# Loads of three value units issued later, four output products moved ahead of a score block, and two x copies put on one engine

## The chip, the cores and the metric

The kernel runs on one core of a Trainium2 chip. The metric is the device time of one launch in microseconds. The engines are TensorE (PE in the profile, with its weight loads as PEld), VectorE (DVE), ScalarE (ACT), GpSimd (POOL) and SyncE (SP), which here only starts DMA transfers. Each engine takes its instructions in the order in which they stand in its own queue, and waits on semaphores for the others.

## The reference

Sliding-window attention is followed by a feed-forward block. q, k and v have 8 batches, 8 heads, 576 positions and 64 elements. Masks keep the scores within 32 positions.

```
scores = scale * (q @ k^T);  scores = -1e9 where |i - j| > 32
attn   = softmax(scores)
x      = (attn @ v), heads side by side         # 4608 tokens x 512
h      = x @ w_in                               # 512 -> 2048
g      = h * sigmoid(1.702 * h)
out    = g @ w_out                              # 2048 -> 512, float32
```

## The kernel before

The 4608 tokens are cut into 36 units of 128 queries and 9 tiles of four units (512 tokens). A unit's queries start 32 positions after its keys, so each unit of queries meets the keys of its own unit and the first half of the next.

**Attention of a unit `u`.** `scores(u, tag)` (or `scores_two` for a pair) multiplies keys and queries into PSUM banks, and ScalarE takes the exponential into `p`. `band` multiplies `p` by the window's mask on VectorE (`band_two` for a pair). `values(u, tag)` multiplies `p` by the values; a ones column gives the softmax sum. `norm` divides on VectorE and leaves the unit in `xn`. `values_four` and `norm_four` do the same for four units. Then x is transposed into `xT`, which is the moving operand of layer one: `x_T2(u, tag, eng)` transposes two units on TensorE into one bank, and the engine `eng` copies them out; `x_T` without a bank asks SP for a DMA transpose. The first three tiles use TensorE, the later ones SP.

**Values.** `load_v(u)` is a DMA issued by GpSimd into one of nine buffers `ve`. The values' second block of 128 keys starts 64 positions later, so `odd_v(u, eng)` makes a copy `vo` shifted by half a unit: its first instruction copies the upper half of `ve[u]`, its second the lower half of `ve[u + 1]`, and so it waits for the load of `u + 1`. Queries and keys of later units come by `load_kq`, also issued by GpSimd (`ahead("kq", u)` loads q of `u` and k of `u + 1`), and `turn` asks SP for their DMA transposes. SP's queue holds, in order, these transposes, the output stores, and the transposes of x.

**Layers one and two.** Both are multiplied by a scheme of seven block products in place of eight (numbers 1 to 7 in the code), with sums of blocks made on VectorE: `x_sums` makes `xs` from `xT`, `g_sums` makes `gs` from `g`. A group of layer one (`l1_group`) takes the banks A, C, B and E; VectorE adds in PSUM (L592, L598), ScalarE copies (L68) and takes the activation (L579). The products of layer two are a list of closures, here called `more` and `l2`, of which `do(more, n)` issues the next `n`. They fill TensorE between dependent steps.

**Order.** The order is written out by hand in `run`, `first_layer1`, `front` and `back`. The change lies between layer one of the second tile (`first_layer1`, units 4 to 7) and that of the third (`back(2)`, units 8 to 11, beside which units 12 to 15 get their values). The PSUM banks are named "A", "B", "C", "E", the double bank "t", and "LA", "LB" for layer two. The probabilities `p` of a pair of units take one of two buffers, so that units 12 and 13 use the one of units 8 and 9 again.

In later stages GpSimd is paced by a copy of one element into the tile `seen`, which makes it wait until that element's tile is written:

```
self.nc.gpsimd.tensor_copy(self.seen, self.gs[t - (n == 0)][0:1, 2, c, 255:256])
```

Of the kernel before, what the change touches and what calls it, by code (L numbers as in the profile page):

```python
# [26 lines left out]
class _Kernel:  # L27
# [844 lines left out]
    @staticmethod  # L872
    def do(fs, n=99):
        for _ in range(min(n, len(fs))):
            fs.pop(0)()
# [76 lines left out]
    def run(self):  # L952
        pool, act = self.nc.gpsimd, self.nc.scalar
        self.l2eng, self.seed2 = self.nc.vector, act
        more = self.l2 = self.layer2_plain(0, 0) + self.layer2([(i, j) for i in range(self.NT) for j in range(2)][1:-1],
                                                               (self.NT - 1, 1))
        self.opening()
        self.do(self.x_sums(1))
        late = self.first_layer1()
        do = self.do  # L960
        dve = self.nc.vector
        do(more, 8)
        self.scores_two(8, ("t", "AC"))
        exps = self.scores(10, "BE", True)
        self.turn(14)
        self.turn(15)
        do(late)
        do(more, 4)
        self.band_two(8)
        self.l2eng = act  # L970
        do(more, 16)
        do(exps)
        do(more, 8)
        self.values(8, "t")
        self.values(9, "AC")
        self.odd_v(12, pool)
        self.odd_v(13, pool)
        self.ahead("kq", 16)
        self.scores(11, "BE")
        self.norm(8)  # L980
        self.band(10)
        self.norm(9)
        do(more, 12)
        self.scores_two(12, ("t", "BE"))
        self.values(10, "AC")
        self.band(11)
        self.norm(10)
        do(more, 6)
        self.values(11, "t")
        self.norm(11)  # L990
        self.scores(14, "BE")
        self.x_T2(8, "A", act)
        do(more, 4)
        self.x_T2(10, "C", dve)
        self.scores(15, "t")
        do(more, 6)
        do(self.x_sums(2))
        self.seed2 = self.l2eng = dve
        self.odd_v(14, pool)
        self.odd_v(15, pool)  # L1000
        late = self.back(2)
        for t in range(3, self.NT):
            self.front(t, late)
            late = self.back(t)
        self.l2eng = act
        self.do(late, 2)
        self.do(self.l2, 16)
        self.do(late)
        self.do(self.l2, 999)

    def first_layer1(self):

        def b(*which):
            return [lambda i=i, j=j: self.w2_sums((i,), j) for i, j in which]

        dv = b((3, 0), (3, 1), (1, 0), (1, 1))
        extra = {0: [lambda: self.w1_sums((4,), 1), lambda: self.g0_sum(1)] + b((2, 0), (2, 1)), 1: b((4, 0), (4, 1)),
                 2: [lambda: self.g0_sum(2)], 3: []}
        for n in range(4):
            self.odd_v(8 + n, self.nc.gpsimd)  # L1020
            self.ahead("kq", 12 + n)
            for u in ((), (), (), (13, 14, 15, 16))[n]:
                self.load_v(u)

            chunks = ((1, 2, 3, 3), (1, 1, 3, 5), (2, 2, 8, 4), (2, 2, 6, 6))[n]
            sums = ((0, 0, 1, 1, 2), (3, 1, 0, 1, 3), (1, 0, 2, 1, 2), (2, 1, 1, 0, 1))[n]

            def fill(i):
                at = (1, 7, 2, 4).index(i)
                self.do(self.l2, chunks[at])  # L1030
                self.do(dv, {1: sums[0], 7: sums[1], 2: 0, 4: sums[4]}[i])
                if i == 7 and n:
                    self.T_pe([("k8", "q8", "k9"), ("q9", "k10", "q10"), ("k11", "q11", "k12")][n - 1], self.nc.scalar)
                    if n == 3:
                        self.turn(12)
                        self.turn(13)

            self.l1_group(1, n, fill, lambda i: self.do(dv, sums[2 + i]))
            dv += self.g_sums(1, 2 * n, 2) + extra[n]
        return dv  # L1040
# [46 lines left out]
```

## Time and profile before

| | us |
|---|---|
| median of 3 runs | 279.73 |
| lowest, highest run | 278.90, 280.01 |
| the profiled execution | 278.88 |
| its span | 277.1 |
| TensorE busy | 265.1 |
| VectorE busy | 213.7 |
| ScalarE busy | 196.1 |
| GpSimd busy | 140.2 |

The span runs from the first to the last record; the execution's own time has 1.78 us around it. In a row of a timeline stand the start, the length, the engine, the line of the kernel, the operation, what it writes and reads, and how many were merged. Idle time ahead of the row and what ended it stand in brackets. Most matmuls have line 71 and most copies line 68, which are helpers, so the tile names tell the steps apart: `sc` are scores, `pv` values, `tp` transposes, `h` layer one, `o` layer two. TensorE's matmuls are pipelined, so that a row's end lies beyond the start of the next. Times are counted from the span's start.

### The profile page before, as it was taken

Reading aid. Unit: us, or ns where it says so; the run is one execution under the profiler, and the core shown is the slowest. Engines: PE = TensorE matmul, PEld = TensorE weight load, DVE = VectorE, ACT = ScalarE, POOL = GpSimd, SP = SyncE. Lnnn points to the kernel's source line nnn. Section 1 sums busy time; section 2 is a strip of 40 time slices with the busy share of each in tenths; the row PEclk is TensorE's granted clock in tenths of the full one; section 3 lists DMA queues with packets and bytes.
Section 4 is the critical chain, followed back from the end, with each engine's and each line's share of the span. In section 5 each row is a group of like instructions: output and inputs, shape, how many; then the busy total and the mean of one; then the engine's idle time right before and its main releaser. Section 6 shows DMA issues by size and latency. Waiting matters only on the chain.

```text
span 277.1 us, 8812 instructions
## 1 busy us (share of the span) xinstructions
PE 265.1 (96%) x3604; PEld 222.4 (80%) x3604; DVE 213.7 (77%) x496; ACT 196.1 (71%) x346; POOL 140.2 (51%) x218
## 2 busy tenths in 40 slices
PE   1989999999999999999999999999999999999994
PEld 1568556888788888888888888888888888888883
DVE  4655998987888788888878887888788878856621
ACT  2586985999896689669956985698569766577320
POOL 8995597999693189729642974294430000000000
PEclk9999999999999999999999999999999999999999
DMA  8999999999999999999999999999992023202033
GB/s 86 165 199 199 180 207 166 164 150 149 188 133 212 163 122 165 173 198 120 171 171 172 151 167 181 134 141 125 153 120 80 0 89 65 78 0 78 0 117 116
DMA packets 151353, 37.74 MB, mean 136 GB/s; under 512 B 138640, under 2 KB 146960, under 8 KB 151312
## 3 DMA queue, kind: packets, MB, share of 16 engines
q0 software_dynamic: 107200, 18.42, 95.4%
q1 hardware_dynamic: 43664, 18.23, 34.3%
q8 instruction: 28, 0.46, 0.7%
q10 hardware_dynamic: 448, 0.52, 0.6%
q14 instruction: 13, 0.11, 0.1%
HBM read 36.83 MB, written 9.44 MB: 167 GB/s over the span
## 4 chain that ended last, share of the span: by engine, by line
PE 93%; ACT 2%; DMA 2%; DVE 1%; issue 1%; POOLq 0%
PE o L71 41%; PE h L71 40%; PE sc L71 5%; PE pv L71 4%; DMA kq<-in_k_dram 2%; PE tp L180 1%; PE tp L259 1%; ACT kq L68 1%; PE tp L463 1%; ACT p L340 1%; DVE xn L398 1%; ACT L803 0%; PE tp L204 0%; DVE kq L68 0%; PE tp L451 0%
## 5 line engine op out<-in xcount | busy, mean ns | idle before, releaser
L579 ACT ACTIVATE g<-h 128x512 f16<-128x512 f32 x128 | 72.1, 598 | 37.9 <-PE h L71 31.6
L71 PEld LDWEIGHTS <-g 128*128 128x128 f16 x568 | 54.6, 98 | 7.7
L71 PE MATMUL h<-xs,a 128*128 128x256 f16 x384 | 57.6, 272 | 0.0
L71 PEld LDWEIGHTS <-a 128*128 128x128 f16 x512 | 49.7, 98 | 8.4 <-DVE xs L495 0.3
L71 PE MATMUL h<-xT,w 128*128 128x256 f16 (+1 forms) x352 | 53.6, 283 | 0.0
L71 PEld LDWEIGHTS <-w 128*128 128x128 f16 x480 | 46.0, 98 | 8.6
L71 PE MATMUL o<-w,g 128*128 128x256 f16 (+1 forms) x304 | 49.9, 284 | 0.0
L233 POOL COPY vo<-ve 64x264 int32<-64x264 int32 x71 | 35.6, 502 | 18.0 <-DMA ve<-in_v_dram 14.5
L71 PEld LDWEIGHTS <-gs 128*128 128x128 f16 x416 | 39.9, 98 | 5.3
L71 PE MATMUL o<-b,gs 128*128 128x256 f16 x280 | 43.3, 273 | 0.0
L71 PE MATMUL o<-b,g 128*128 128x256 f16 x264 | 38.6, 273 | 0.0
L592 DVE TENSOR_TENSOR h<-h,s 128x512 f32<-128x512 f32 x32 | 22.4, 699 | 18.8 <-PE h L71 18.2
L214 POOL DMA_DIRECT2D ve<-in_v_dram x39 | 33.2, 864 | 2.5 <-issue 1.2
L144 POOL DMA_DIRECT2D qst<-in_q_dram x35 | 28.2, 808 | 1.3 <-issue 0.9
L598 DVE TENSOR_TENSOR h<-h,s 128x512 f32<-128x512 f32 x32 | 22.3, 698 | 7.3 <-PE h L71 7.1
L144 POOL DMA_DIRECT2D kst<-in_k_dram x31 | 26.6, 861 | 1.4 <-DMA w<-in_moe_w_out_dram 1.4
L68 ACT COPY h<-h 128x512 f32<-128x512 f32 x32 | 18.8, 587 | 10.4 <-PE h L71 9.6
L293 ACT ACTIVATE p<-sc 128x512 bf16<-128x512 f32 x48 | 24.7, 623 | 0.3 <-PE sc L71 0.2
L943 POOL COPY seen<-gs 1x1 f16<-1x1 f16 x17 | 3.3, 196 | 36.9 <-DVE gs L510 36.9
L68 ACT COPY o_sb<-o 128x256 f32<-128x256 f32 (+1 forms) x25 | 11.7, 467 | 12.6 <-PE o L71 12.6
L68 ACT COPY s<-h 128x512 f32<-128x512 f32 x32 | 19.1, 598 | 0.8
L71 PE MATMUL h<-xs,w 128*128 128x256 f16 x128 | 19.2, 273 | 0.0
(101 smaller groups left out, 389.0 us busy)
## 6 DMA issues: line engine op xcount, KB each, us to landing
out_dram<-o_sb SPq DMA_DIRECT2D x33, 256.0 KB, 4.1
ve<-in_v_dram POOLq DMA_DIRECT2D x31, 128.0 KB, 6.5
kst<-in_k_dram POOLq DMA_DIRECT2D x25, 128.0 KB, 5.7
qst<-in_q_dram POOLq DMA_DIRECT2D x21, 128.0 KB, 5.2
w<-in_moe_w_out_dram POOLq DMA_DIRECT2D x4, 512.0 KB, 10.6
w<-in_moe_w_in_dram POOLq DMA_DIRECT2D x4, 256.0 KB, 8.5
w<-in_moe_w_in_dram POOLq DMA_DIRECT2D x2, 512.0 KB, 10.6
qst<-in_q_dram POOLq DMA_DIRECT2D x7, 96.0 KB, 5.8
```

The source lines that it names most:

```text
L68: (eng.copy if eng is self.nc.scalar else eng.tensor_copy)(out, in_)
L71: self.nc.tensor.matmul(out, lhsT, rhs, start=start, stop=stop, skip_group_check=True)
L144: self.nc.gpsimd.dma_start(t[off:off + n], src[b, :, s:s + n, :].rearrange("h s d -> s h d"))
L180: self.nc.tensor.transpose(tp[64 * (h % 2):64 * (h % 2) + 64, h // 2, x, :], src[:, 4 * i + h, at + x, :], self.ident[r, r])
L214: self.nc.gpsimd.dma_start(t[off:off + n, :, :self.D], self.v[b, :, s:s + n, :].rearrange("h s d -> s h d"))
L233: eng.tensor_copy(*((words(vo[64:128]), words(self.ve[u % 9][64:128])), (words(vo[0:64]), words(nxt)))[i])
L259: self.nc.tensor.transpose(tp[:, i, hp, :], src[:, 128 * hp:128 * hp + 128], self.ident)
L293: exps = [lambda eo=eo: self.nc.scalar.activation(p[:, eo].rearrange("k h s -> k (h s)"), sc[eo], AF.Exp, scale=self.scale) for eo in rang ...
L579: act.activation(g[:, f, 256 * half:256 * half + 256], bank.rearrange("p (i n) -> p i n", i=2), AF.Gelu_apprx_sigmoid)
L592: dve.tensor_add(e, b, s7)
L598: dve.tensor_add(c, b, s7)
L943: self.nc.gpsimd.tensor_copy(self.seen, self.gs[t - (n == 0)][0:1, 2, c, 255:256])
```

## The change

The change has three parts.

The loads of values 14, 15 and 16 are issued later. They stood right behind that of 13 at the end of `first_layer1`. Now GpSimd first makes the odd copy of unit 12, copies one element of the masked probabilities of units 8 and 9 into `seen`, and then issues them, followed by q of 16 and k of 17. The odd copy of unit 13 moves behind those, to the odd copies of 14 and 15.

Four products of layer two, which stood between the two x copies of the third tile, are issued ahead of the scores of unit 14.

The copy of units 8 and 9 out of bank A goes to VectorE, where that of units 10 and 11 was already.

```
         self.values(9, "AC")
         self.odd_v(12, pool)
-        self.odd_v(13, pool)
-        self.ahead("kq", 16)
         self.scores(11, "BE")
         self.norm(8)
+        pool.tensor_copy(self.seen, self.pair[8][0:1, 0, 1, 0, 0:1])
+        for u in (14, 15, 16):
+            self.load_v(u)
+        self.ahead("kq", 16)
         self.band(10)
...
         self.norm(11)
+        do(more, 4)
         self.scores(14, "BE")
-        self.x_T2(8, "A", act)
-        do(more, 4)
+        self.x_T2(8, "A", dve)
         self.x_T2(10, "C", dve)
         self.scores(15, "t")
         do(more, 6)
         do(self.x_sums(2))
         self.seed2 = self.l2eng = dve
-        self.odd_v(14, pool)
-        self.odd_v(15, pool)
+        for u in (13, 14, 15):
+            self.odd_v(u, pool)
...
-            for u in ((), (), (), (13, 14, 15, 16))[n]:
+            for u in ((), (), (), (13,))[n]:
                 self.load_v(u)
```

GpSimd's queue around the end of `first_layer1`, with the difference marked. The tiles `ve_86` to `ve_89` hold the values of units 13 to 16, `ve_85` those of 12; `vo_93` is the odd copy of 12, and `vo_94` that of 13.

```order
-L214 DMA ve_87<-in_v_dram 128x8x64
-L214 DMA ve_88<-in_v_dram 128x8x64
-L214 DMA ve_89<-in_v_dram 128x8x64
 L233 COPY vo_93<-ve_85 64x264
 L233 COPY vo_93<-ve_86 64x264
+L979 CAST seen<-p 1x1
+L214 DMA ve_87<-in_v_dram 128x8x64
+L214 DMA ve_88<-in_v_dram 128x8x64
+L214 DMA ve_89<-in_v_dram 128x8x64
+L144 DMA qst<-in_q_dram 128x8x64
+L144 DMA kst<-in_k_dram 128x8x64
 L233 COPY vo_94<-ve_86 64x264
```

The three loads of values stand behind the odd copy of unit 12 and the new copy into `seen`, and the loads of q and k now stand ahead of the odd copy of unit 13.

TensorE's queue at the end of the values of unit 11 (`vo_92` is its odd copy) and the start of the scores of unit 14, with the difference marked:

```order
 L71 LDWEIGHTS p
 L71 MATMUL pv<-vo_92,p 64x65
+L71 LDWEIGHTS g
+L71 MATMUL o<-b_79,g 128x256
+L71 LDWEIGHTS g
+L71 MATMUL o<-b_79,g 128x256
+L71 LDWEIGHTS g
+L71 MATMUL o<-b_79,g 128x256
+L71 LDWEIGHTS g
+L71 MATMUL o<-b_79,g 128x256
 L71 LDWEIGHTS kT
 L71 MATMUL sc<-qT,kT 64x64
```

The four products with their weight loads now come between the values and the scores; the same eight instructions are gone from between the transposes of units 8 and 9 and those of 10 and 11.

VectorE's queue from the last norm before layer one of the third tile, with the difference marked:

```order
 L397 RECIPROCAL rec<-pv 128x8
 L398 TENSOR_TENSOR xn<-pv,rec 128x512
-L68 COPY xT<-tp 128x2x4x128
+L68 COPY xT<-tp 128x2x4x128 x2
 L495 TENSOR_TENSOR xs<-xT 128x512 x2
 L495 TENSOR_TENSOR xs<-xT,xs 128x512
 L496 TENSOR_TENSOR xs<-xT,xs 128x512
 L678 TENSOR_TENSOR o_sb<-o,s7o 128x256
```

Two copies of x now stand ahead of the x sums, where one did; ScalarE's queue loses the other.

## The prediction

> **What bounds the kernel now.** I read the page first, then the chain of waits, then the timelines of the engines between 62 and 105 us, where the change acts.
>
> ```profile
> span 277.1 us, 8812 instructions
> PE 265.1 (96%) x3604; PEld 222.4 (80%) x3604; DVE 213.7 (77%) x496; ACT 196.1 (71%) x346; POOL 140.2 (51%) x218
> PE 93%; ACT 2%; DMA 2%; DVE 1%; issue 1%; POOLq 0%
> ```
>
> TensorE is busy for 96% of the span and 93% of the chain is its work. A change that adds no matmul can only win what TensorE idles, and loses only what it makes TensorE wait for. The execution took 278.88 us, 1.78 more than its span. The chain of waits from 58 to 90 us shows one place where it leaves TensorE:
>
> ```profile
> 74.19 0.62 ACT p L340
> 74.86 0.41 PE sc L71 x13
> ```
>
> ScalarE's last exponential of units 12 and 13 ends at 74.81, and the scores of unit 14 go on at 74.86: they need bank E, which that exponential reads. TensorE's own rows there, as starts:
>
> ```profile
> 70.42 0.48 PE L71 MATMUL sc<-qT,kT 64*64 64x64 bf16 x24
> 70.83 1.05 PE L71 MATMUL o<-b,gs 128*128 128x256 f16 x8
> 71.72 0.60 PE L71 MATMUL o<-w,g 128*128 128x256 f16 x4
> 72.25 0.74 PE L71 MATMUL sc<-q_two,kT 64*64 64x64 bf16 x40
> ...
> 74.43 0.25 PE L71 MATMUL sc<-qT,kT 64*64 64x64 bf16 x3
> 74.86 0.41 PE L71 MATMUL sc<-qT,kT 64*64 64x64 bf16 x21 [0.18 <-ACT p L340]
> 75.20 0.62 PE L463 MATMUL tp<-identh,xn 128*128 128x128 f16 x8
> 75.66 0.60 PE L71 MATMUL o<-b,g 128*128 128x256 f16 x4
> 76.10 0.61 PE L463 MATMUL tp<-identh,xn 128*128 128x128 f16 x8
> 76.64 0.45 PE L71 MATMUL sc<-qT,kT 64*64 64x64 bf16 x24
> 77.02 0.39 PE L71 MATMUL o<-b,g 128*128 128x256 f16 x2
> ```
>
> The reader is to see the three matmuls at 74.43 and the next at 74.86. The page's ends overlap the next starts, so I work with starts. 24 scores take 0.41 (70.42 to 70.83); here they take 0.77 (74.43 to 75.20). So the hole is 0.36 us. The changed order puts work into it that stood elsewhere.
>
> **The change, part by part.** *Four products ahead of the scores of unit 14.* From 74.43 on, the new row is: four products followed by scores, 0.53 (71.72 to 72.25); 24 scores, 0.41; the eight transposes of the first x copy, 0.46 (75.20 to 75.66); the eight of the second and the turn to scores, 0.54 (76.10 to 76.64); scores of unit 15, 0.38 (76.64 to 77.02). That is 2.32 us and ends at 76.75, against 77.02 before: **0.27 us won**. It is less than the hole of 0.36, since four products ahead of scores cost 0.53 where they cost 0.44 ahead of transposes (75.66 to 76.10). The scores now start at 74.96, 0.15 after bank E is free, so the wait is gone. What could be late next is the norm of unit 11, whose transposes now start at 76.07 (75.83 and half of 0.46):
>
> ```profile
> 75.08 0.69 DVE L398 TENSOR_TENSOR xn<-pv,rec 128x512 f16<-128x512 f32 x1
> 76.75 0.69 DVE L68 COPY xT<-tp 128x1024 f16<-128x1024 f16 x1 [0.97 <-PE tp L463]
> 77.47 0.78 DVE L495 TENSOR_TENSOR xs<-xT 128x512 f16<-128x512 f16 x2
> ...
> 79.19 0.42 DVE L678 TENSOR_TENSOR o_sb<-o,s7o 128x256 f32<-128x256 f32 x1
> 79.81 0.70 DVE L592 TENSOR_TENSOR h<-h,s 128x512 f32<-128x512 f32 x1 [0.19 <-PE h L71]
> ```
>
> It ends at 75.77, 0.3 earlier, so it does not wait.
>
> *Both x copies on VectorE.* The first copy went to ScalarE between two pairs of exponentials:
>
> ```profile
> 72.75 2.06 ACT L340 ACTIVATE p<-sc 128x512 bf16<-128x512 f32 x4 [0.74 <-PE sc L71]
> 76.26 1.02 ACT L68 COPY xT<-tp 128x1024 f16<-128x1024 f16 x1
> 77.16 1.11 ACT L293 ACTIVATE p<-sc 128x512 bf16<-128x512 f32 x2
> 78.37 0.57 ACT L68 COPY h<-h 128x512 f32<-128x512 f32 x1
> ```
>
> ScalarE drops about 0.9 us (76.26 to 77.16), so the exponentials of unit 15 follow their scores at 76.75 and end near 77.9. The bank copy at 78.37 needs the first layer-one product, then 0.27 earlier, at 78.10, so ScalarE holds nothing. VectorE gains a copy of 0.69. The second copy stood at 76.75, 0.65 after the start of its transposes at 76.10. By that lag the first copy starts at 75.38 + 0.65 = 76.03 and ends at 76.72; the second, whose transposes allow 76.48, starts behind it and ends near 77.36, where it ended at 77.44. With the small overlaps of neighbouring rows I take the x sums as 0.1 earlier, not 0.27. VectorE then sat idle for 0.19 before the add at 79.81, so that add can come at 79.62 - 0.1 = 79.52, and TensorE, 0.27 ahead, asks for it at 79.54. The copy costs nothing, with almost no spare: if VectorE loses more than 0.02 there, the gain shrinks by that.
>
> *Values 14 to 16 held back.* GpSimd's rows:
>
> ```profile
> 65.14 4.02 POOL L214 DMA_DIRECT2D ve<-in_v_dram  x5
> ...
> 70.38 0.40 POOL L233 COPY vo<-ve 64x264 int32<-64x264 int32 x1 [0.42 <-DMA ve<-in_v_dram]
> ...
> 74.05 0.88 POOL L144 DMA_DIRECT2D qst<-in_q_dram  x1
> ...
> 75.85 1.78 POOL L233 COPY vo<-ve 64x264 int32<-64x264 int32 x4
> 77.59 1.37 POOL L144 DMA_DIRECT2D qst<-in_q_dram  x2
> ...
> 87.04 0.18 POOL L943 COPY seen<-gs 1x1 f16<-1x1 f16 x1 [3.70 <-DVE gs L510]
> DMA to landing us min/median/max: 5.1/6.9/7.4
> ```
>
> The last row is that of the five loads at 65.14. The mark comes behind the odd copy that ends at 70.78, and the mask that it waits for is done before that:
>
> ```profile
> 69.00 0.69 DVE L347 TENSOR_TENSOR p<-p,mask 128x1024 bf16<-128x1024 bf16 x1 [0.29 <-ACT p L340]
> 87.23 0.22 PE L71 MATMUL pv<-ve,p 128*64 128x65 bf16 x1
> ```
>
> So the mark itself makes nobody wait, but the three loads move from 66.5 to about 71.3 (the mark at 87.04 was 0.49 ahead of the next issue). At 0.88 each they end at 73.9, and the queries and keys behind them end near 75.7, as before. The odd copies of 13 to 15 follow and now wait for landings. The last one needs unit 16, issued at 73.05: landed at 78.2 to 80.4 by the 5.1 to 7.4 above. I take 79, since the later place has fewer loads queued just ahead. The last copy ends near 79.5, not 77.6: six loads behind it (77.59 onward) come 1.9 later, with bounds 0.9 to 3.7. GpSimd idled for 3.7 before 87.04, which takes that up, and the values of units 12 to 15, at 87.23, still have 6 us or more.
>
> What those six loads feed is SP's queue. Its transposes of queries and keys stand ahead of those of x for the fourth tile, and all move with the loads:
>
> ```profile
> 92.61 5.16 SPq L447 DMA_TRANSPOSE xT<-xn  x4
> DMA to landing us min/median/max: 3.3/4.0/4.5
> 103.26 0.42 DVE L495 TENSOR_TENSOR xs<-xT 128x512 f16<-128x512 f16 x1
> 104.51 0.60 PE L71 MATMUL h<-xs,a 128*128 128x256 f16 x4
> ```
>
> The fourth starts near 96.5 and lands by 101.0; the first x sum wants it at 103.26, or 103.0 with the gain. Spare: 2.0 before VectorE waits, some 0.8 more before TensorE does at 104.51. A shift of 1.9 costs nothing. Nor do I credit the quieter DMA queues at 66 to 69 us with anything: no row of TensorE there waits for a transfer.
>
> *GpSimd's copies beside VectorE's x sums.* The odd copies now lie at about 76 to 79.5, across the x sums (77.4 to 79). What that costs, by rows:
>
> ```profile
> 60.43 0.62 DVE L507 TENSOR_TENSOR gs<-g 128x512 f16<-128x512 f16 x1
> 104.38 0.51 DVE L495 TENSOR_TENSOR xs<-xT,xs 128x512 f16<-128x512 f16 x1
> ```
>
> Both have 0.42 elsewhere and stood beside odd copies. So one of the four sums loses 0.09 or, at the worst row, 0.20: bounds 0 to 0.8. I take one loss of 0.09, since 104.38 is the same operation. Less the spare of 0.02 that costs TensorE 0.07. The Trainium skill (SBUF — State Buffer, "Who interferes with whom") says that a VectorE operation with two SBUF inputs and a GpSimd operation that reads SBUF exclude each other for a whole instruction. By it each of four sums could wait out a copy, some 0.4 as at 70.38, which makes 1.6 where my sum has 0.09; the row at 60.43 neither reaches that nor contradicts it.
>
> **The sum.** -0.27 + 0.07 = -0.20 us: 278.7 against the profiled 278.88. That execution lies 0.85 under the median, 279.73, so as a median I forecast **279.5**.
>
> **The rivals.**
> 1. *VectorE is late.* The odd copies strike all four x sums: 4 x 0.20 = 0.8. The adds of the first layer-one group, and TensorE behind them, are late by 0.78, net +0.5: 280.2. It decides once VectorE loses over 0.3. For it: VectorE has no spare there. Against: four such sums with two odd copies near 104 lost 0.09 once. The exclusion rule above at its full 1.6 would give +1.3: 281.0.
> 2. *x of the fourth tile is late; slower than before.* If landings take 7.4 and the copies are slow, GpSimd's shift is 3.7; TensorE waits 3.7 - 2.8 = 0.9 at 104, net +0.7: 280.4. It decides from a shift of 2.8. For it: the median landing of 6.9. Against: it takes the slowest landing of the five and a copy twice as long as that at 70.38, with nothing now queued just ahead.
> 3. *The mark holds ScalarE.* It reads the probabilities of units 8 and 9, whose buffer units 12 and 13 reuse, so the exponentials at 72.75 now stand behind it. It ends near 71.0 if the load of unit 13 lands by 70.3 as before; only beyond 1.75 later does it cost, up to about 0.5, net +0.2: 279.9.
> 4. *The hole simply moves*, by a wait for a copied x: 279.7.
>
> **How the numbers follow.** The forecast, a gain of 0.1 to 0.36, gets 0.55; rival 1 0.12, rival 2 0.10, rival 3 0.04, rival 4 0.10, and 0.09 stays for what no row shows. The range runs from the lowest run, 278.9, less the whole hole, to the highest, 280.01, with rival 2's wait: 278.5 to 281.0. A measurement of this kernel can tell about 0.5%, 1.4 us, from no change. No case but rival 1 by the rule, rivals added up, or the unseen comes to that: slower 0.10, faster 0.03, same 0.87.
>
> **What would show it.** Right: no wait for ScalarE's exponential ahead of the scores of unit 14, the products after unit 15's scores 0.2 to 0.3 earlier, and the same lead at 104 us. Wrong: VectorE's add of the first group waited for by TensorE; x sums of 0.5 to 0.8; GpSimd's last odd copy after 80.5; the x sum of the fourth tile waiting for SP's transposes; exponentials of units 12 and 13 waiting for GpSimd.

## The result and the profile after

The changed kernel takes 280.91 us, the median of 11 runs (279.42 to 282.78), against 279.17 for the kernel before in 11 runs. The ratio is 1.0065, with a 95% interval of 1.0039 to 1.0091. So it is slower by 0.65%. The profiled execution took 280.49 us. The profiles of the experiments e3, e4 and e9 fell on disturbed executions and are not read below; the ratios leave such runs out, the medians do not.

The page of the kernel after:

```profile
span 278.7 us, 8814 instructions
PE 265.3 (95%) x3604; PEld 221.6 (80%) x3604; DVE 213.9 (77%) x497; ACT 195.3 (70%) x345; POOL 140.1 (50%) x219
PE 87%; DMA 6%; DVE 2%; ACT 2%; POOL 1%; issue 1%; POOLq 0%; DVEq 0%
```

TensorE has the same work (265.3 us against 265.1) in a span that is 1.6 us longer. Part of the chain is now a transfer, `xT<-xn`. TensorE's timeline where the products were moved:

```profile
74.79 0.61 PE L71 MATMUL o<-b,g 128*128 128x256 f16 x4
75.33 0.45 PE L71 MATMUL sc<-qT,kT 64*64 64x64 bf16 x24
75.71 1.07 PE L463 MATMUL tp<-identh,xn 128*128 128x128 f16 x16
76.71 0.44 PE L71 MATMUL sc<-qT,kT 64*64 64x64 bf16 x24
77.09 0.39 PE L71 MATMUL o<-b,g 128*128 128x256 f16 x2
```

The hole is filled. From 74.79 to 77.09 it takes 2.30 us, where the same work took 2.59 before. Counted from the beginning, this execution was 0.43 us late at 70 us, by chance in the opening (the same kernel in e12 was 0.02 early there), and 0.07 late at 77: 0.36 won. It stays 0.08 late up to 104 us. Then come these rows, of SP, GpSimd (two), VectorE, TensorE, the chain of waits, and the landings of the x transposes:

```profile
93.67 5.85 SPq L447 DMA_TRANSPOSE xT<-xn  x4
95.80 0.18 POOL L943 COPY seen<-gs 1x1 f16<-1x1 f16 x1 [6.35 <-DVE gs L510]
96.26 2.63 POOL L214 DMA_DIRECT2D ve<-in_v_dram  x3 [0.29 <-issue]
105.42 0.42 DVE L495 TENSOR_TENSOR xs<-xT 128x512 f16<-128x512 f16 x1 [2.00 <-DMA xT<-xn]
105.90 0.61 PE L71 MATMUL h<-xs,a 128*128 128x256 f16 x4 [1.15 <-DVE xs L495]
98.30 7.03 DMA xT<-xn
DMA to landing us min/median/max: 3.9/5.7/7.0
```

VectorE waits 2.0 us for the fourth tile's x, and TensorE for VectorE. The last x transpose starts at 98.30, 1.76 later than before, and lands at 105.3, 7.0 us after its start, where the longest took 4.5 before. The loads of values 17 to 19 (the row at 96.26) follow a mark that waits for a block sum of VectorE, not for the lateness of GpSimd's queue, and start where they did before:

```profile
96.19 2.63 POOL L214 DMA_DIRECT2D ve<-in_v_dram  x3 [0.29 <-issue]
```

Behind the wait at 104 us TensorE is 1.54 late, and 1.61 at the end. GpSimd's rows say where the lateness began:

```profile
69.79 0.59 POOL L233 COPY vo<-ve 64x264 int32<-64x264 int32 x1 [2.95 <-DMA ve<-in_v_dram]
70.34 0.18 POOL L979 CAST seen<-p 1x1 f16<-1x1 bf16 x1
70.46 2.65 POOL L214 DMA_DIRECT2D ve<-in_v_dram  x3
73.08 0.91 POOL L144 DMA_DIRECT2D qst<-in_q_dram  x1
...
76.84 0.86 POOL L233 COPY vo<-ve 64x264 int32<-64x264 int32 x2 [0.61 <-DMA ve<-in_v_dram]
78.51 0.67 POOL L233 COPY vo<-ve 64x264 int32<-64x264 int32 x1 [0.81 <-DMA ve<-in_v_dram]
79.13 1.37 POOL L144 DMA_DIRECT2D qst<-in_q_dram  x2
```

The odd copies wait twice for landings, and the six loads of queries and keys behind them begin at 79.13 where they began at 77.59.

### The profile page after: what moved, and what is told of

It is laid out like the page before. It is cut to its first block, busy times and chain, and to the rows that moved or that the text cites. A ratio compares the mean times of both kernels' runs of the same rounds, so it can differ in the third digit from the quotient of the medians.

```text
span 278.7 us, 8814 instructions
## 1 busy us (share of the span) xinstructions
PE 265.3 (95%) x3604; PEld 221.6 (80%) x3604; DVE 213.9 (77%) x497; ACT 195.3 (70%) x345; POOL 140.1 (50%) x219
## 3 DMA queue, kind: packets, MB, share of 16 engines
q0 software_dynamic: 107200, 18.42, 96.6%
## 4 chain that ended last, share of the span: by engine, by line
PE 87%; DMA 6%; DVE 2%; ACT 2%; POOL 1%; issue 1%; POOLq 0%; DVEq 0%
PE o L71 39%; PE h L71 37%; PE sc L71 5%; PE pv L71 4%; DMA o_sb<-in_k_dram 4%; DMA xT<-xn 3%; PE tp L180 1%; PE tp L259 1%; ACT kq L68 1%; PE tp L463 1%; POOL kq L155 1%; ACT L803 0%; POOL vo L233 0%; PE tp L204 0%; DVE xn L398 0%
```

## The experiments

Theory A: GpSimd's odd copies wait for the held back values and hold the loads of queries and keys behind them; SP's x transposes of the fourth tile come late and run into the loads of values 17 to 19. Its rivals were that the x copies and products do it (B), that the held back loads crowd the queues (C), and, within A, that lateness alone suffices (A2) where A1 says that it takes the collision with those loads.

### e1: the loads as before

```
-for u in ((), (), (), (13,))[n]:
+for u in ((), (), (), (13, 14, 15, 16))[n]:
```

with the odd copies and `ahead("kq", 16)` back in place. The products and x copies stay changed.

> The change without its first part: loads of values 14 to 16 and the odd copy of 13 stand where they stood before; the four products stay ahead of the scores of unit 14 and both x copies on VectorE. Theory A (the loss is the fourth tile's x being late, because GpSimd's queue is late): no wait at 104 us, the hole at 74.5 filled, 0.3 to 0.36 us faster than before, about 278.85 against 279.17. Rival B (the loss comes from the x copies on VectorE or the moved products, through what they do to the later order): still slower than before by 1 us or more.

279.34 us, ratio 1.0005 (0.9986 to 1.0024), and no wait at 104 us. So B falls: the products and copies are not what makes it slower. But the gain is missing too. TensorE shows a new hole at 79 us with no releaser:

```profile
80.06 0.38 PE L71 MATMUL o<-b,gs 128*128 128x256 f16 x2 [0.76 <-issue]
```

### e2: the loads alone

```
-do(more, 4); scores(14); x_T2(8, "A", dve)
+scores(14); x_T2(8, "A", act); do(more, 4)
```

> The load part alone: values 14 to 16 held back as in the change, products and x copies as before. Theory A: TensorE waits some 1.2 to 1.5 us at 104 for the fourth tile's x, and nothing is won at 74.5: 1.0 to 2.0 us slower than before, about 280.7 to 281.2. Rival B: the same time as before within 0.3 us.

280.38 us, ratio 1.0032 (1.0006 to 1.0059): slower by 0.9 us by the ratio, a little less than expected. The profiled execution has the wait at 104, and runs from 278.59 to 283.04 us suggest that its size differs from run to run. Rows of TensorE and SP:

```profile
106.28 0.61 PE L71 MATMUL h<-xs,a 128*128 128x256 f16 x4 [1.41 <-DVE xs L495]
95.29 5.29 SPq L447 DMA_TRANSPOSE xT<-xn  x4
```

### e3: values 17 to 19 one step earlier

```
-LOADS = {(2, 1): [("kq", 8)], (2, 2): [("v", 5, 6, 7)], ...
+LOADS = {(2, 1): [("kq", 8), ("v", 5, 6, 7)], (2, 2): [], ...
```

> The change with one more edit: the three loads of values 17 to 19, which GpSimd issues at 96 to 99 us, are issued one step earlier, behind q of 20 and k of 21 at 89 us. GpSimd's lateness of 1.5 us at 79 and SP's of 1.8 us at 96 stay. Theory A1 (the lateness alone would have been hidden by the spare of 2.8 us; the x transposes became slow, 7.0 us to landing where it was 4.5, since they now run beside those three loads): the last landing is back near 4 to 5 us, no wait of TensorE at 104, 0.2 to 0.4 us faster than before. Rival A2 (SP's lateness alone does it, the collision does not matter): the wait at 104 stays over 1 us, slower than before by 0.7 us or more.

281.68 us in the median, ratio 1.0048 (1.0022 to 1.0074). A1's expectation missed, and the time alone would fit A2. But the edit was a poor test: by the order of the queues it puts the same three loads beside other transposes of SP, and the time can't tell that from A2. e6 asks the question again.

### e4 and e7: the odd copies behind the loads of q and k

```
 self.ahead("kq", *((17,), (18, 19), (), ())[n])
+for i in ((), (13, 14, 15), (), ())[n]:
+    self.odd_v(i, self.nc.gpsimd)
```

and those copies gone from `run`.

> The change with the odd copies of 13 to 15 issued behind the loads of queries 17 to 19 and keys 18 to 20 instead of ahead of them; values 14 to 16 still held back. Theory A (those copies wait for landings and hold the loads behind them): the six loads start near 74.9 instead of 79.1, SP's transposes run without a late start, no wait at 104, 0.2 to 0.4 us faster than before. Rival C (the held back loads themselves crowd the DMA queues, whatever GpSimd's order): TensorE still waits at 104 by 0.5 us or more.

> The same kernel as e4, whose profile fell on a run with a lowered clock, for a profile and more runs. Theory A: no wait at 74.5 nor at 104, SP's x transposes start no later than 92.6 and the last lands within 5 us; 0.2 to 0.4 us faster than before. Rival C: a wait at 104.

279.20 us, ratio 0.999 (0.9974 to 1.0005), and again 279.38 us, ratio 1.0009 (0.9991 to 1.0026). In e7's profile there is no wait at 104, and SP's x transposes start at 92.83; the last lands 3.9 us after its start. So C falls, for the values are still held back. Yet there is no gain: a small hole at 78 us, and a wait at 85. Rows of SP, VectorE, GpSimd and TensorE of e7:

```profile
92.83 5.15 SPq L447 DMA_TRANSPOSE xT<-xn  x4
81.64 2.36 DVE L367 TENSOR_TENSOR p<-p,mask 128x1024 bf16<-128x1024 bf16 x3
83.93 0.62 DVE L507 TENSOR_TENSOR gs<-g 128x512 f16<-128x512 f16 x1
84.58 0.51 DVE L508 TENSOR_TENSOR g<-g 128x512 f16<-128x512 f16 x1
81.44 3.92 POOL L233 COPY vo<-ve 64x264 int32<-64x264 int32 x6
85.75 0.60 PE L71 MATMUL h<-xs,a 128*128 128x256 f16 x4 [0.48 <-DVE h L592]
```

The six odd copies now lie beside VectorE's bands and block sums, which take 3.49 us by these three rows. VectorE is late, and TensorE with it.

### e5: GpSimd late, and nothing else

```
-self.odd_v(14, pool); self.odd_v(15, pool)
+for u in (14, 15, 14, 15):
+    self.odd_v(u, pool)
```

in the kernel before.

> The kernel before with four more odd copies on GpSimd (14 and 15 made twice), 4 x 0.445 = 1.8 us, ahead of the loads of queries 17 to 19: nothing else of the change is in it, the values are loaded where they stood. Theory A (GpSimd's lateness at 79 us is enough): SP's x transposes of the fourth tile come 1.5 to 2 us later, run into the loads of values 17 to 19, and TensorE waits 0.5 to 1.7 us at 104; 0.5 to 1.7 us slower than before. Rival C (the held back value loads crowd the queues): no wait at 104, the same as before within 0.3 us.

279.52 us, ratio 1.002 (0.9999 to 1.004): 0.3 us slower between the medians and some 0.6 by the ratio, at or under the low end of what A expected, and the interval just reaches no change. The times alone show nothing; how often the wait comes in the other runs is not known. The profiled execution (280.10 us) shows it. Rows of SP, GpSimd and TensorE:

```profile
93.51 5.59 SPq L447 DMA_TRANSPOSE xT<-xn  x4
96.10 2.63 POOL L214 DMA_DIRECT2D ve<-in_v_dram  x3 [0.29 <-issue]
105.71 0.61 PE L71 MATMUL h<-xs,a 128*128 128x256 f16 x4 [1.12 <-DVE xs L495]
```

With the values loaded where they always were, and GpSimd's queue made late, the wait at 104 is there.

### e6: without the loads of values 17 to 19

```
-(2, 2): [("v", 5, 6, 7)],
+(2, 2): [],
```

in the changed kernel; units 17 to 19 then use old values.

> The change with the loads of values 17 to 19 left out, so that those units use old values (part of the computation is missing); GpSimd's mark at 96 us and its lateness at 79 stay. Theory A1 (lateness needs the collision with these three loads): SP's x transposes still start 1.5 to 2 us late, but the last lands within 4 to 5 us, at about 102.5 to 103; no wait of TensorE at 104; 0.3 us faster than before in the lead at 110 us. Rival A2 (lateness alone): the wait at 104 stays at 1 us or more.

278.99 us, ratio 0.9993 (0.9972 to 1.0015). SP and VectorE:

```profile
93.82 6.04 SPq L447 DMA_TRANSPOSE xT<-xn  x4
DMA to landing us min/median/max: 2.5/4.1/5.0
103.14 0.42 DVE L495 TENSOR_TENSOR xs<-xT 128x512 f16<-128x512 f16 x1
```

SP is as late as in the changed kernel (the last transpose starts at 98.64 against 98.30), but the last one lands 4.4 us after its own start, and nobody waits. A2 falls: lateness alone was hidden, as the spare said. It needs the collision.

The expected lead of 0.3 us at 110 was missed: TensorE is 0.42 ahead of before at 78 us, but only 0.12 from 79 on. Up to there the order is that of the changed kernel, but in this execution GpSimd's six odd copies lie across all four x sums of the third tile. Rows of GpSimd, VectorE and TensorE:

```profile
77.14 3.04 POOL L233 COPY vo<-ve 64x264 int32<-64x264 int32 x6
77.20 1.17 DVE L495 TENSOR_TENSOR xs<-xT 128x512 f16<-128x512 f16 x2
78.40 0.51 DVE L495 TENSOR_TENSOR xs<-xT,xs 128x512 f16<-128x512 f16 x1
78.94 0.51 DVE L496 TENSOR_TENSOR xs<-xT,xs 128x512 f16<-128x512 f16 x1
78.57 0.27 PE L71 MATMUL o<-w,g 128*128 128x256 f16 x1
78.97 0.61 PE L71 MATMUL h<-xs,a 128*128 128x256 f16 x4
```

The four sums take 2.19 us by these rows, against 1.62 before (0.78, 0.42 and 0.42). The third ends at 78.91, and TensorE's product that reads the sums starts at 78.97, behind a hole of 0.29.

### e8: e1 again

> The same kernel as e1, for a second profile. If the wait for the keys of unit 16 at 76.7 (0.2 us) and the hole without a releaser at 79 (0.9 us) in its first profile belong to this kernel, they are there again and the time equals before. If they are chance, TensorE is 0.3 us ahead of before from 77 us on.

279.53 us, ratio 0.9994 (0.9969 to 1.0019). The hole is there again, in front of the same matmul, with no wait for unit 16's keys this time:

```profile
79.17 0.38 PE L71 MATMUL o<-b,gs 128*128 128x256 f16 x2 [0.63 <-issue]
```

### e9: the odd copies between the loads

```
-self.ahead("kq", *((17,), (18, 19), (), ())[n])
+self.ahead("kq", *((17,), (), (), ())[n])
+for i in ((13, 14, 15), (), (), ())[n]:
+    self.odd_v(i, self.nc.gpsimd)
+self.ahead("kq", *((), (18, 19), (), ())[n])
```

> The change with the odd copies of 13 to 15 between the loads for unit 17 and those for 18 and 19: values still held back, products and x copies as in the change. Theory A: the loads of q 18 to k 20 run when they ran before (79.8 to 83.3), SP's last x transpose starts less than 1.1 us behind the first load of values 17 to 19, no wait at 104. Theory D (the odd copies hurt where they lie beside VectorE's bands and block sums at 81 to 85): here they are done by 80, so no wait at 85 either. Then at most 0.36 us ahead of before, the time 0 to 0.15% under it. Rival: any wait of 0.3 us or more at 78, 85 or 104 eats it.

279.56 us, ratio 1.0007 (0.9989 to 1.0024). It does not beat the kernel before. Where its gain went is open.

### e10: e4 without the odd copies of 13 to 15

```
-for i in ((), (13, 14, 15), (), ())[n]:
+for i in ((), (), (), ())[n]:
```

> The kernel e4 with the odd copies of units 13 to 15 left out, so that those units use old copies (part of the computation is missing). Theory D (those copies, beside VectorE's three bands and two block sums at 81.6 to 85.1, made them take 3.49 us where they took 2.73 before, and TensorE waited 0.65 us at 85): the wait at 85 is gone and the bands are back to 1.9 us for three. Rival: the wait at 85 has another cause and stays.

The copies are left out, so units 13 to 15 use old ones. One execution, 279.21 us. VectorE:

```profile
82.01 1.89 DVE L367 TENSOR_TENSOR p<-p,mask 128x1024 bf16<-128x1024 bf16 x3
83.81 0.42 DVE L507 TENSOR_TENSOR gs<-g 128x512 f16<-128x512 f16 x1
84.27 0.42 DVE L508 TENSOR_TENSOR g<-g 128x512 f16<-128x512 f16 x1
```

2.73 us where e7 had 3.49, and no wait at 85. The odd copies cost e7 that wait. The Trainium skill (SBUF — State Buffer, "Who interferes with whom") says that VectorE operations with two SBUF inputs and GpSimd's reads of SBUF exclude each other; these two traces agree that the operations are slower beside the copies, at 0.1 to 0.2 us an operation, and show none that waits out a whole copy.

### e11: e1 without the loads of values 14 to 16

```
-for u in ((), (), (), (13, 14, 15, 16))[n]:
+for u in ((), (), (), (13,))[n]:
```

> The kernel e1 with the loads of values 14 to 16 left out (part of the computation is missing): the same order on TensorE, fewer transfers at 66 to 76 us. Theory F (at 78 us TensorE cannot go past its matmul 1113 before its instructions are fetched: the transfer of the instruction queue came at 76.6 and 77.6 in e1's two runs against 76.2 before, late by the crowd of loads, and TensorE went on 1.4 to 1.6 us after its end): the transfer comes earlier, by 76.2, and the hole at 78 to 79 is under 0.2 us. Rival: the hole stays near 0.8 us with a transfer that ended over 1.7 us before.

Units 14 to 16 use old values. One execution, 278.60 us. The transfer of instructions before the hole (the tables below list it) started at 74.3, and the hole is gone:

```profile
78.42 0.38 PE L71 MATMUL o<-b,gs 128*128 128x256 f16 x2
```

This execution is 0.35 us ahead of before from 77 us on and 0.28 at the end. It shows, in one trace, the gain that the moved products can bring when the transfer is early. That the three loads are what makes it late is not shown: in e6, with those loads in place, it started at 74.8.

### e12: the change again

> The changed kernel again, for a second profile. Theory A1: if SP's last x transpose starts more than 1.5 us behind the first load of values 17 to 19, it lands 6 us or more after its start and TensorE waits over 0.5 us at 104; if less than 1.1 us behind, no wait. Theory F: where matmul 1113 waits, it goes on 1.4 to 1.6 us after the end of the instruction transfer before it.

One execution, 280.25 us, with both effects in one trace: a hole of 0.52 at 78, and the wait at 104:

```profile
105.63 0.61 PE L71 MATMUL h<-xs,a 128*128 128x256 f16 x4 [0.81 <-DVE xs L495]
```

### The traces side by side

The last x transpose of the fourth tile, and the first load of values 17 to 19 (us). The hole is the spacing of TensorE's starts at 104, less the usual 0.11:

```
kernel    load    transpose  behind  lands   after start  hole at 104
e7        96.61   96.76      0.15    100.67  3.9          none
e10       96.46   96.67      0.21    101.09  4.4          none
e11       95.83   96.12      0.29    100.57  4.4          none
before    96.19   96.54      0.35    101.07  4.5          none
e1        97.46   98.34      0.88    103.06  4.7          none
e8        96.57   97.60      1.03    102.56  5.0          none
e12       96.33   98.02      1.69    105.05  7.0          0.97
e5        96.10   97.80      1.70    105.14  7.3          1.28
change    96.26   98.30      2.03    105.32  7.0          1.31
e2        96.38   99.29      2.91    105.71  6.4          1.57
e6        none    98.64      -       103.02  4.4          none
```

The table has the last of the four transposes alone. The third is drawn in too: it took 6.5 us when it started 0.72 behind the first load (the change) and 7.1 when 1.53 behind (e2), against 2.4 in the kernel before, where it ran ahead, and 2.5 in e6.

The hole at 78 to 79 us in front of one and the same product, the instruction transfer before it (one packet of 16 KB on the queue that the page calls instruction), and that product (e6's hole, three matmuls further on, is VectorE's):

```
kernel    transfer ends  TensorE goes on  between  hole
e1        78.64          80.06            1.42     0.92
e8        77.61          79.17            1.56     0.79
e12       77.51          78.91            1.40     0.52
e10       77.65          78.98            1.33     0.41
e5        77.21          78.70            1.49     0.35
e7        77.19          78.61            1.42     0.23
before    77.23          78.77            1.54     none
e2        77.20          78.97            1.77     none
change    76.97          78.84            1.87     none
e6        75.71          78.35            2.64     none
e11       75.28          78.42            3.14     none
```

## Why the prediction was wrong

It forecast a gain of 0.2 us and the kernel lost 1.7. That 280.91 lies in the stated range is luck: the range's upper end was the highest run of before with rival 2's wait, and that rival asked for other causes. One sign that it named for being wrong came: the x sum of the fourth tile waits for SP's transposes. By its own steps:

**The four products.** Right. 0.27 was forecast by starts, and the two traces' rows give 2.59 - 2.30 = 0.29. That they are kept is another matter (the unseen, below).

**Both x copies on VectorE.** Right. VectorE's add came at 79.88, 0.43 of which is that execution's late opening; 79.52 was forecast. In this trace rival 1 did not happen, and of the four x sums one lost 0.09, as assumed:

```profile
78.95 0.51 DVE L496 TENSOR_TENSOR xs<-xT,xs 128x512 f16<-128x512 f16 x1
79.88 0.70 DVE L592 TENSOR_TENSOR h<-h,s 128x512 f32<-128x512 f32 x1
```

But how many sums are struck depends on when the copies run: in e12, the same kernel, two lost 0.09 each, and in e6, where the copies lay across all four, they lost 0.57 in all and TensorE waited 0.29. That is within the bounds of 0 to 0.8, and rival 1 in small; the 1.6 of full exclusion was not seen. In e7 the same effect came where the copies lay beside the bands.

**GpSimd's shift.** Right: 1.54 (1.97 in e12, 2.54 in e6) where 1.9 was taken, with bounds 0.9 to 3.7. Nobody waited for the mark, so rival 3 did not happen either.

**SP's spare.** This step failed, in one term. SP's last x transpose came 1.76 later, close to the 1.9, and the spare of 2.8 would have hidden that, as e6 shows. But the spare counted a landing of 4.5 us, read where three transposes ran ahead of the loads of values 17 to 19 and the last started 0.35 behind the first of them. Those loads do not move with GpSimd's shift: they follow the mark on VectorE's block sum, and start at 95.8 to 96.6 in every trace of the table that has them but e1's, where TensorE was 1.28 late. So a late transpose does not only start later, it starts among them, and lands after 7.0. That is 1.76 + 2.5 = 4.3 against a spare of 2.8: 1.5 us of wait, and TensorE lost 1.46 (from 0.08 to 1.54 late), 1.31 of it in the hole itself. Rival 2 named the place and the order of events, but asked for a shift of GpSimd by 2.8, from slow landings of values and slow copies; 1.54 was enough for the transposes to fall among the loads.

**The unseen.** The hole at 78 was in no row of the trace before, where the transfer's end was 1.54 ahead of the product that needs it. Six traces go on 1.33 to 1.56 after the transfer's end when they have the hole, and the five without it 1.54 or more. So in no trace does the product start sooner than 1.33 us after the transfer, and a gain ahead of it is returned there when the transfer is late. e5, in which no product was moved, was 0.42 us ahead at 78 by its opening, and has the hole too. The first trace of the changed kernel has none because its late opening had taken the lead; e12 gave back 0.52. e11 agrees: an earlier transfer, no hole, and the gain kept. That the transfer carries just this product's instructions is inferred from its queue's name and from these intervals; no run showed it directly, nor what sets the time of the transfer.

No version here beats the kernel before beyond its interval. With loads as before (e1, e8), or the copies moved (e4, e7, e9), the ratios lie between 0.9990 and 1.0009. That the two parts alone (1.0005 and 1.0032) seem to give less than the whole is within their intervals.

## What to carry to other kernels

When a change makes a transfer later, ask what it will then run beside, and whether those neighbours move with it: a spare read from landings ahead of a burst is no spare among the burst. In a queue that both issues loads and copies their results, a copy that waits for a landing holds every load behind it; put the loads that feed a distant step ahead of it, and look at what the copies then lie beside. A hole that is filled on the bounding engine is a gain only until its next fixed date, here, as it seems, the transfer of its own instructions.

## What the runs showed of the hardware

The last of four DMA transposes of x issued by SP landed within 5.0 us of its start when that was up to 1.03 us behind the first of three loads of 128 KB each by GpSimd; 1.69 us or more behind it took 6.4 to 7.3. Without the loads one that started as late took 4.4. The third of the four was slow (6.5 us) from 0.72 behind, so the distance to the first load alone sets no bound.

The profile lists a queue with 28 packets of 16 KB:

```profile
q8 instruction: 28, 0.46, 0.7%
```

One of them started between 74.3 and 77.6 us in these traces, and where the profile marks the hole of TensorE that follows its end, it is as "issue", without a releaser.

VectorE's four x sums, 1.62 us in all, took 2.19 where GpSimd's odd copies lay across all of them (e6). Its bands and block sums took 0.1 to 0.2 us more an operation beside those copies (e7) than without them (e10).
